# Two output tiles moved to the last phase of a two-branch attention kernel, and its closing steps put in another order

## The chip, the cores and the metric

The kernel runs on one core of a Trainium2 chip. The metric is the device time of one execution in microseconds. A core has a matrix engine (PE, with its weight loads listed apart as PEld), a vector engine (DVE), a scalar engine (ACT), GpSimd (POOL) and a sync engine (SP), which here issues every DMA. Each works through its own list of instructions in order, and they wait for each other by semaphores.

## The reference

Two attention branches over 2048 tokens, each 640 wide with 32 heads of 20 columns, side by side in the output. Branch A works in four segments of 512 tokens with a memory that is carried from one to the next; branch B has a sliding window of 256.

```python
# branch A, segment s (L = 512); M, z start at zero
p = softmax(qs @ ks.T * scale + causal_mask)
a_dot = p @ vs
a_mem = (phi(qs) @ M) / (phi(qs) @ z + 1e-6)      # phi(t) = t + 1 if t > 0 else exp(t)
o = g * a_mem + (1 - g) * a_dot                   # g = sigmoid(beta), one per head
M = M + phi(ks).T @ vs;  z = z + phi(ks).sum(tokens)
out_A = concat(o) @ wo

# branch B
mask = (i - j >= 0) & (i - j < 256)
out_B = softmax(where(mask, q @ k.T * scale, -1e9)) @ v @ wo

out = concat([out_A, out_B], axis=-1)
```

## The kernel before

The work is cut into chunks of 512 tokens and runs in eight **phases**, in the order B0, A0, B1, A1, B2, A2, B3, A3 (branch and chunk). The fourth phase is A1, the sixth A2, the seventh B3 and the last A3. A phase is a list of **packs**, 20 of them (24 in B1 to B3). A pack is one call of `scores`: PE writes the scores of four heads into two PSUM tiles called `Sc` (three buffers), ACT takes their exponential into `pt` with two instructions (L465), and POOL clears the masked blocks. The packs of all phases are counted by `slot`.

Around the packs, all other work is placed by a planner in `body`. Each kind of step has a cost in it: 0.45 a pack, 1.19 a projection of queries or keys (`proj`, L267), 0.79 half a projection of values (`vproj`, L326), 0.4 a step of the memory (`read`, L435, and `upd`, L402), 0.75 a sum of values for four heads (`weigh`, L514), and 0.75 half an output tile (`out_half`, L580). The planner adds these up to a total for the phase, and after each pack `pick` chooses how many of the next projections, memory steps and output halves to emit, so that the cost placed so far follows the share of the phase that is done. The projections of a phase are those of the next chunk, so the last phase has none.

All of these steps put their PSUM result into tiles called `D`, of which there are two buffers, and DVE takes nearly all of these results out, so PE and DVE hand the two buffers back and forth. A sum (`weigh`) of one group of four heads is copied to `oc` by DVE (L527), turned by a DMA transpose into `ocT`, and some packs later normalised (L544, L549) into `otA` or `otB`, the tokens' rows of a chunk; in branch A the memory's part `omem` is added (L561).

An **output tile** is 128 tokens of a chunk and a branch. `prefetch` issues a DMA transpose for it (L571, tile `oT`, up to three tiles under way), and at least two packs later `out_step` emits its halves: five matmuls with the weights `Ao` or `Bo` into a `D` tile and a DVE copy to `ot` (L583); behind the second half stands the store (L587). `OUT_TILES` says how many tiles each phase takes. There are 28 tiles of the first seven phases; the last phase asks for eight and gets the seven that are left. The four tiles of the last phase itself are made in the end, `tail`.

**The end** begins in the last pack. `last_turn` turns the first three of the five blocks of `otA` on PE (L616) ahead of that pack's scores and copies them to `pkt` (`oTs`, L623); after the pack `tail` emits, in this order: the sum of the last group but one (`weigh(u)`), its DVE copy, the last masks on DVE (L744), then for tile 0 the partial output over three of five blocks (`last_mm`, L628), the transposes of that sum on PE (`turn_here`, L536) and its normalisation, the partial output of tile 1, the last sum (`weigh(w)`), whose copy is split between ACT (L522) and DVE (L523), the partial output of tile 2, the transposes of the last sum and its normalisation. Then `last_turn` turns the last two blocks (L616) and copies them, half by DVE (L620) and half by ACT (L621). Three tiles are completed (two more blocks each), copied by ACT or DVE (L641, L643) and stored; the fourth is done whole, in an `Sc` tile, copied by DVE (640 columns) and stored by SP.

Of the kernel before, what the change touches and what calls it, by code (L numbers as in the profile page):

```python
# [9 lines left out]
BF16 = mybir.dt.bfloat16  # L10
F32 = mybir.dt.float32

P = 128
S = 2048
D = 640
# [4 lines left out]
KT = 5  # L20
NC = 4
CH = 512
CT = CH // P
# [1 line left out]
EPS = 1e-6  # L25
SCALE = float(DH) ** -0.5
LAG = 2
OUT_TILES = (0, 0, 3, 2, 6, 3, 7, 8)
VW = 22


# [51 lines left out]
class Kern:  # L83
# [411 lines left out]
    def weigh(self, u):  # L495
        nc = self.nc
        O = self.dtile([P, CH], F32)
        written = [False] * CT
        jobs = []
        for (_, kt, off, q0, nq), pt in u.work:  # L500
            runs = []
            for b in range(nq):
                w = written[q0 + b]
                if runs and runs[-1][2] == w:
                    runs[-1][1] += 1
                else:
                    runs.append([b, 1, w])
                written[q0 + b] = True
            jobs += [(kt, off + b, q0 + b, nb, pt) for b, nb, _ in runs]
        for n, (kt, off, q0, nq, pt) in enumerate(jobs):  # L510
            v = self.vt[u.br][(kt // CT) % 2 if u.br == "B" else 0]
            for j in range(4):
                v0 = VW * (4 * u.g + j)
                nc.tensor.matmul(O[32 * j:32 * j + 32, q0 * P:(q0 + nq) * P],  # L514
                                 lhsT=v[:, kt % CT, v0:v0 + 32],
                                 rhs=pt[:, j, off * P:(off + nq) * P],
                                 start=(n == 0), stop=(n == len(jobs) - 1),
                                 tile_position=(0, 32 * j))
        oc = self.wk.tile([P, CH], BF16, name="oc", bufs=2)
        if self.closing:  # L520
            if u.g == G - 1:
                nc.scalar.copy(out=oc[:, 0:256], in_=O[:, 0:256])  # L522
                nc.vector.tensor_copy(out=oc[:, 256:512], in_=O[:, 256:512])  # L523
            else:
                nc.vector.tensor_copy(out=oc[:], in_=O[:])
            return oc
        nc.vector.tensor_copy(out=oc[:], in_=O[:])  # L527
        tp = self.wk.tile([P, CT, P], BF16, name="ocT", bufs=4)
        nc.sync.dma_start_transpose(out=tp[:], in_=oc[:])
        late = 3 if u.br == "A" and u.c == NC - 1 else 4  # L530
        self.at(self.slot + late, lambda: self.normalise(u, tp))

    def turn_here(self, u, oc):
        tp = self.dtile([P, CT, P], BF16)
        for b in range(CT):
            self.nc.tensor.transpose(out=tp[:, b, :], in_=oc[:, b * P:(b + 1) * P],  # L536
                                     identity=self.ident[:])
        self.normalise(u, tp)

# [65 lines left out]
    def last_turn(self, br, c, m0, m1):  # L605

        nc = self.nc
        o = self.o_tok[br, c]
        if m0 == 0:
            self.oTs = self.wk.tile([P, KT, CT, P], BF16, name="pkt", bufs=1)  # L610
        n = 2 if m0 == 0 else 4
        for a in range(0, CT, n):
            ps = self.dtile([P, m1 - m0, n, P], BF16)
            for i in range(n):
                for m in range(m0, m1):
                    nc.tensor.transpose(out=ps[:, m - m0, i, :],  # L616
                                        in_=o[:, a + i, m * P:(m + 1) * P],
                                        identity=self.ident[:])
            if m0:
                nc.vector.tensor_copy(out=self.oTs[:, m0:m1, 0:2, :], in_=ps[:, :, 0:2, :])  # L620
                nc.scalar.copy(out=self.oTs[:, m0:m1, 2:4, :], in_=ps[:, :, 2:4, :])  # L621
            else:
                nc.vector.tensor_copy(out=self.oTs[:, m0:m1, a:a + 2, :], in_=ps[:])  # L623

    def last_mm(self, br, tt, m0, m1):
        for hf in range(2):
            for m in range(m0, m1):
                self.nc.tensor.matmul(self.last[tt][hf], lhsT=self.oTs[:, m, tt, :],  # L628
                                      rhs=self.w[br + "o"][:, m, hf * 320:(hf + 1) * 320],
                                      start=(m == 0), stop=(m == KT - 1))  # L630

# [4 lines left out]

    def last_store(self, br, c, tt, ps, eng):
        nc = self.nc
        ot = self.wk.tile([P, 2, 320], BF16, name="ot" if tt < 3 else "oT", bufs=3 if tt < 3 else 4)
        if eng is nc.scalar:  # L640
            nc.scalar.copy(out=ot[:], in_=ps[:, :, 0:320])  # L641
        else:
            nc.vector.tensor_copy(out=ot[:], in_=ps[:, :, 0:320])  # L643
        r0 = c * CH + tt * P
        c0 = 0 if br == "A" else D
        nc.sync.dma_start(out=self.out2d[r0:r0 + P, c0:c0 + D],
                          in_=ot[:].rearrange("p a b -> p (a b)"))

# [5 lines left out]
    def body(self):  # L656
# [4 lines left out]
        for n, ph in enumerate(phases):  # L661
            dense = lists[n]
            mem = []
            if ph.br == "A" and ph.c > 0:
                mem = [(0.4, lambda tt=tt, hf=hf: self.read(ph.c, tt, hf))
                       for hf in range(2) for tt in range(CT)] + upd[ph.c]
            outs = 2 * OUT_TILES[n]
            np_ = len(ph.packs)
# [67 lines left out]
    def tail(self, br, c):  # L736

        nc = self.nc
        self.closing, self.last, ps = True, {}, {}
        (_, u), (_, w) = self.ready  # L740
        assert not self.tiles
        ou = self.weigh(u)
        for blk in self.open_masks:
            nc.vector.tensor_tensor(out=blk, in0=blk,  # L744
                                    in1=self.cmask[:].unsqueeze(1).to_broadcast([P, 2, P]),
                                    op=ALU.mult)
        while self.turned or self.half:
            self.out_step()
        while self.after or self.behind:
            for f in self.after.pop(self.slot, []) + self.behind.pop(self.slot, []):  # L750
                f()
            self.slot += 1
        ps[0] = self.last_sc(0)
        self.last_mm(br, 0, 0, 3)
        self.turn_here(u, ou)
        ps[1] = self.last_sc(1)
        self.last_mm(br, 1, 0, 3)
        ow = self.weigh(w)
        ps[2] = self.last_sc(2)
        self.last_mm(br, 2, 0, 3)  # L760
        self.turn_here(w, ow)
        self.last_turn(br, c, 3, KT)
        for tt in range(3):
            self.last_mm(br, tt, 3, KT)
            self.last_store(br, c, tt, ps[tt], (nc.scalar, nc.vector)[tt % 2])
        ps[3] = self.last_sc(3)
        self.last_mm(br, 3, 0, KT)
        self.last_store(br, c, 3, ps[3], nc.vector)


@with_exitstack
# [47 lines left out]
```

## Time and profile before

| what | us |
|---|---|
| median of 3 runs | 392.48 (390.49 to 394.0) |
| the profiled execution | 390.19 |
| its span, first to last instruction | 388.1 |
| PE busy | 340.4 (88%) |
| ACT busy | 338.1 (87%) |
| DVE busy | 276.7 (71%) |
| POOL busy | 251.8 (65%) |

The span is what the profiler saw between the first and the last instruction of the core; the profiled execution's own time is 2.1 us more. "Busy" sums the time of an engine's instructions, and an average over the whole span says little here, since the phases differ in what sets their pace. In a line of waits, the engine and line before the arrow sat idle until the one behind it was done; the numbers are the total in us, how often, and the longest. In a line of the timeline stand the start, the duration, the engine, the line of the kernel, the operation and its output and input, the number of instructions that are merged in it, and in brackets the engine's idle time before it with what ended that.

### The profile page before, as it was taken

Reading aid. Unit: us, or ns where it says so; the run is one execution under the profiler, and the core shown is the slowest. Engines: PE = TensorE matmul, PEld = TensorE weight load, DVE = VectorE, ACT = ScalarE, POOL = GpSimd, SP = SyncE. Lnnn points to the kernel's source line nnn. Section 1 sums busy time; section 2 is a strip of 40 time slices with the busy share of each in tenths; the row PEclk is TensorE's granted clock in tenths of the full one; section 3 lists DMA queues with packets and bytes.
Section 4 is the critical chain, followed back from the end, with each engine's and each line's share of the span. In section 5 each row is a group of like instructions: output and inputs, shape, how many; then the busy total and the mean of one; then the engine's idle time right before and its main releaser. Section 6 shows DMA issues by size and latency. Waiting matters only on the chain.

```text
span 388.1 us, 10554 instructions
## 1 busy us (share of the span) xinstructions
PE 340.4 (88%) x4060; PEld 161.3 (42%) x4060; DVE 276.7 (71%) x581; ACT 338.1 (87%) x384; POOL 251.8 (65%) x392
## 2 busy tenths in 40 slices
PE   7999988977998798988997989898999989988884
PEld 3433434322443344444543335444454435544442
DVE  2467667634788868788778886789877887777583
ACT  2867789985999889888999999988999999999972
POOL 9657564542777587635578888844458988955550
PEclk9999999998999989999999999999999999999999
DMA  8993328647434597728575697758474377736312
GB/s 256 314 285 77 47 83 151 113 105 187 134 80 134 143 173 141 135 71 137 117 135 135 127 190 126 149 104 110 116 146 120 92 169 129 113 78 113 96 30 70
DMA packets 110738, 50.77 MB, mean 131 GB/s; under 512 B 81760, under 2 KB 110688, under 8 KB 110688
## 3 DMA queue, kind: packets, MB, share of 16 engines
q1 hardware_dynamic: 110688, 50.10, 61.1%
q8 instruction: 32, 0.52, 0.6%
q14 instruction: 18, 0.15, 0.1%
HBM read 16.39 MB, written 14.42 MB: 79 GB/s over the span
## 4 chain that ended last, share of the span: by engine, by line
PE 42%; ACT 24%; DVE 16%; issue 6%; POOL 6%; DMA 3%; SPq 0%; POOLq 0%; DVEq 0%; ACTq 0%
ACT pt L465 22%; PE D L267 13%; PE Sc L459 7%; PE D L326 6%; PE D L580 5%; PE D L514 5%; PE D L253 4%; POOL pt L479 3%; DVE qk L270 3%; POOL pt L485 3%; DVE oc L527 3%; ACT pe L310 2%; PE Sc L628 2%; DVE omem L445 1%; DMA ocT<-oc 1%
## 5 line engine op out<-in xcount | busy, mean ns | idle before, releaser
L465 ACT ACTIVATE pt<-Sc 128x1024 bf16<-128x1024 f32 (+1 forms) x344 | 320.7, 1077 | 32.3 <-PE Sc L459 28.2
L479 POOL TENSOR_SCALAR_AFFINE_SELECT pt<-pt 128x512 bf16<-128x512 bf16 x254 | 167.6, 671 | 117.2 <-ACT pt L465 116.9
L485 POOL TENSOR_SCALAR_AFFINE_SELECT pt<-pt 128x512 bf16<-128x512 bf16 x112 | 78.6, 717 | 5.1 <-ACT pt L465 4.8
L270 DVE CAST qk<-D 128x512 bf16<-128x512 f32 x70 | 47.9, 687 | 29.4 <-PE D L267 26.8
L527 DVE CAST oc<-D 128x512 bf16<-128x512 f32 x62 | 42.7, 688 | 19.9 <-PE D L514 19.8
L459 PE MATMUL Sc<-qpB,kpB 20*128 20x256 bf16 (+2 forms) x704 | 43.3, 277 | 7.8 <-ACT pt L465 4.7
L459 PE MATMUL Sc<-qpA,kpA 20*128 20x384 bf16 (+3 forms) x512 | 41.0, 302 | 5.8 <-ACT pt L465 5.0
L580 PEld LDWEIGHTS <-oT 128*128 128x128 bf16 x280 | 25.4, 98 | 17.9 <-issue 6.6
L583 DVE CAST ot<-D 128x320 bf16<-128x320 f32 x56 | 27.0, 485 | 7.2 <-PE D L580 6.4
L459 PEld LDWEIGHTS <-kpB 20*128 20x128 bf16 x704 | 13.6, 92 | 42.5 <-issue 38.5
L267 PE MATMUL D<-xTA,Aq 128*128 128x512 bf16 x100 | 24.9, 379 | 4.6 <-DVE oc L527 3.5
L326 PE MATMUL D<-Av,xTA 128*128 128x320 bf16 x160 | 26.2, 300 | 2.8 <-DVE vA L334 1.6
L514 PE MATMUL D<-pt,vA 128*32 128x256 bf16 (+3 forms) x576 | 23.5, 287 | 5.7 <-DVE qk L270 2.2
L580 PE MATMUL D<-Bo,oT 128*128 128x320 bf16 x160 | 27.3, 306 | 1.0 <-DVE omem L445 0.4
L267 PE MATMUL D<-xTA,Ak 128*128 128x512 bf16 x100 | 25.3, 384 | 2.1 <-DVE qk L270 2.0
L326 PE MATMUL D<-Bv,xTB 128*128 128x320 bf16 x160 | 26.0, 300 | 1.4 <-DVE oc L527 0.9
L514 PE MATMUL D<-pt,vB 128*32 128x384 bf16 (+2 forms) x720 | 26.1, 277 | 0.5 <-DVE qk L270 0.3
L459 PEld LDWEIGHTS <-kpA 20*128 20x128 bf16 x512 | 11.7, 91 | 30.6 <-issue 27.9
L267 PE MATMUL D<-xTB,Bq 128*128 128x512 bf16 x75 | 19.8, 396 | 3.4 <-DVE qk L270 3.2
L549 DVE TENSOR_TENSOR otB<-ocT,rr 128x320 bf16<-128x320 bf16 x32 | 20.2, 631 | 1.1
L544 DVE RECIPROCAL rr<-ocT 128x16 f32<-128x16 bf16 x62 | 15.1, 243 | 8.0 <-DMA ocT<-oc 8.0
L580 PE MATMUL D<-Ao,oT 128*128 128x320 bf16 x120 | 20.1, 299 | 0.7 <-DVE qk L270 0.4
(84 smaller groups left out, 358.8 us busy)
## 6 DMA issues: line engine op xcount, KB each, us to landing
out_dram<-ot SPq DMA_DIRECT2D x31, 160.0 KB
kdA<-qk SPq DMA_DIRECT2D x20, 128.0 KB
qdA<-qk SPq DMA_DIRECT2D x20, 128.0 KB
kdB<-qk SPq DMA_DIRECT2D x15, 128.0 KB
qdB<-qk SPq DMA_DIRECT2D x15, 128.0 KB
kpB<-kdB SPq DMA_DIRECT2D x8, 160.0 KB
qpB<-qdB SPq DMA_DIRECT2D x8, 160.0 KB
kpA<-kdA SPq DMA_DIRECT2D x8, 160.0 KB
```

The source lines that it names most:

```text
L267: nc.tensor.matmul(ps[:], lhsT=self.w[br + which][:, kt, m * P:(m + 1) * P], rhs=self.xT[br][:, kt, :], start=(kt == 0), stop=(kt == KT - 1))
L270: nc.vector.tensor_copy(out=t[:], in_=ps[:])
L326: nc.tensor.matmul(ps[:, 0:320], lhsT=self.xT[br][:, kt, tt * P:(tt + 1) * P], rhs=self.w[br + "v"][:, kt, hf * 320:(hf + 1) * 320], start ...
L459: nc.tensor.matmul(ps[j // 2][:, j % 2, off * P:(off + nq) * P], lhsT=kp[rows, u.g, k0:k0 + P], rhs=self.qp[u.br][rows, u.g, q0 * P:(q0 + ...
L465: nc.scalar.activation(out=pt[:, 2 * hp:2 * hp + 2, 0:pk.used], in_=ps[hp][:, :, 0:pk.used], func=ACT.Exp, scale=SCALE)
L479: nc.gpsimd.affine_select(out=blk, in_=blk, pattern=[[0, 4], [1, P]], compare_op=ALU.is_ge, fill=0.0, base=0, channel_multiplier=-1)
L485: nc.gpsimd.affine_select(out=blk, in_=blk, pattern=[[0, 4], [-1, P]], compare_op=ALU.is_ge, fill=0.0, base=-1, channel_multiplier=1)
L514: nc.tensor.matmul(O[32 * j:32 * j + 32, q0 * P:(q0 + nq) * P], lhsT=v[:, kt % CT, v0:v0 + 32], rhs=pt[:, j, off * P:(off + nq) * P], star ...
L527: nc.vector.tensor_copy(out=oc[:], in_=O[:])
L549: nc.vector.tensor_tensor(out=o[:, :, cols].rearrange("p b (j e) -> p b j e", j=4), in0=pv[:, :, :, 0:DH], in1=rr[:].unsqueeze(3).to_broad ...
L580: nc.tensor.matmul(ps[:, 0:320], lhsT=st["oT"][:, m, :], rhs=self.w[br + "o"][:, m, hf * 320:(hf + 1) * 320], start=(m == 0), stop=(m == K ...
L583: nc.vector.tensor_copy(out=st["ot"][:, hf * 320:(hf + 1) * 320], in_=ps[:, 0:320])
```

## The change

Two numbers of `OUT_TILES` go down by one: the fourth phase takes one tile (two before), the sixth two (three). The last phase asks for ten instead of eight and gets the nine that are left.

In the end, five things change. The last sum stands right behind the transposes of the sum before it, ahead of the partial output of tile 1; that partial output is split, its first half ahead of the transposes of the last sum and its second half behind them, where the partial output of tile 2 also goes. The two halves of the last sum's copy go to two tiles. ACT's half of the copy of the last two blocks goes to a tile of its own (`oTl`, a buffer that was used for `phik`), and `last_mm` takes these blocks from there for tiles 2 and 3. The last output tile is made by the new `last_tile`: two halves in `D` tiles, the first copied by DVE and stored by SP, the second copied by ACT and stored by a DMA that ACT issues.

```diff
-OUT_TILES = (0, 0, 3, 2, 6, 3, 7, 8)
+OUT_TILES = (0, 0, 3, 1, 6, 2, 7, 10)
...
             if u.g == G - 1:
+                o2 = self.wk.tile([P, CH], BF16, name="oc", bufs=2)
                 nc.scalar.copy(out=oc[:, 0:256], in_=O[:, 0:256])
-                nc.vector.tensor_copy(out=oc[:, 256:512], in_=O[:, 256:512])
...
+                nc.vector.tensor_copy(out=o2[:, 256:512], in_=O[:, 256:512])
+                return [oc, oc, o2, o2]
...
+        else:
+            t = self.wk.tile([P, CH], BF16, name="phik", bufs=3)
+            self.oTl = t[:].rearrange("p (m i q) -> p m i q", m=2, i=2)
...
-                nc.scalar.copy(out=self.oTs[:, m0:m1, 2:4, :], in_=ps[:, :, 2:4, :])
+                nc.scalar.copy(out=self.oTl, in_=ps[:, :, 2:4, :])
...
-    def last_mm(self, br, tt, m0, m1):
-        for hf in range(2):
+    def last_mm(self, br, tt, m0, m1, halves=(0, 1)):
+        for hf in halves:
             for m in range(m0, m1):
-                self.nc.tensor.matmul(self.last[tt][hf], lhsT=self.oTs[:, m, tt, :],
+                oT = self.oTl[:, m - 3, tt - 2, :] if m > 2 and tt > 1 else self.oTs[:, m, tt, :]
+                self.nc.tensor.matmul(self.last[tt][hf], lhsT=oT,
...
+    def last_tile(self, br, c):
+
+        nc = self.nc
+        ps = [self.dtile([P, CH], F32) for _ in range(2)]
+        self.last[CT - 1] = [p[:, 0:320] for p in ps]
+        r0 = c * CH + (CT - 1) * P
+        c0 = 0 if br == "A" else D
+        for hf in range(2):
+            self.last_mm(br, CT - 1, 0, KT, (hf,))
+            ot = self.wk.tile([P, KT, P], BF16, name="oT", bufs=4)
+            ot = ot[:].rearrange("p m q -> p (m q)")[:, 0:320]
+            if hf == 0:
+                nc.vector.tensor_copy(out=ot, in_=ps[hf][:, 0:320])
+            else:
+                nc.scalar.copy(out=ot, in_=ps[hf][:, 0:320])
+            (nc.sync, nc.scalar)[hf].dma_start(
+                out=self.out2d[r0:r0 + P, c0 + 320 * hf:c0 + 320 * hf + 320], in_=ot)
...
         self.turn_here(u, ou)
+        ow = self.weigh(w)
         ps[1] = self.last_sc(1)
-        self.last_mm(br, 1, 0, 3)
-        ow = self.weigh(w)
+        self.last_mm(br, 1, 0, 3, (0,))
+        self.turn_here(w, ow)
+        self.last_mm(br, 1, 0, 3, (1,))
         ps[2] = self.last_sc(2)
         self.last_mm(br, 2, 0, 3)
-        self.turn_here(w, ow)
         self.last_turn(br, c, 3, KT)
         for tt in range(3):
             self.last_mm(br, tt, 3, KT)
             self.last_store(br, c, tt, ps[tt], (nc.scalar, nc.vector)[tt % 2])
-        ps[3] = self.last_sc(3)
-        self.last_mm(br, 3, 0, KT)
-        self.last_store(br, c, 3, ps[3], nc.vector)
+        self.last_tile(br, c)
```

More of the change, by code (lines that the diff above doesn't have):

```diff
@@ L521, in weigh @@
             if u.g == G - 1:
+                o2 = self.wk.tile([P, CH], BF16, name="oc", bufs=2)
                 nc.scalar.copy(out=oc[:, 0:256], in_=O[:, 0:256])
[L523 to L526, printed above, removed]
+                nc.vector.tensor_copy(out=o2[:, 256:512], in_=O[:, 256:512])
+                return [oc, oc, o2, o2]
+            nc.vector.tensor_copy(out=oc[:], in_=O[:])
+            return [oc] * CT
         nc.vector.tensor_copy(out=oc[:], in_=O[:])
@@ L535, in turn_here @@
         for b in range(CT):
-            self.nc.tensor.transpose(out=tp[:, b, :], in_=oc[:, b * P:(b + 1) * P],
+            self.nc.tensor.transpose(out=tp[:, b, :], in_=oc[b][:, b * P:(b + 1) * P],
                                      identity=self.ident[:])
@@ L638, in last_store @@
         nc = self.nc
-        ot = self.wk.tile([P, 2, 320], BF16, name="ot" if tt < 3 else "oT", bufs=3 if tt < 3 else 4)
+        ot = self.wk.tile([P, 2, 320], BF16, name="ot", bufs=3)
         if eng is nc.scalar:
```

## The prediction, made before the changed kernel had run

> **What bounds the kernel now.** I read the page first, then busy time by phase, then who waited for whom inside each phase, then the chain of waits, and last the timeline of the end. A pack is one `scores` call: two exp activations on ACT. Counting back from the last of the 344 exps gives the phase limits: the fourth phase runs from 157.30 to 198.85 us, the sixth from 249.00 to 291.30, the seventh to about 338.30, the eighth to 375.50.
>
> ```profile
> span 388.1 us, 10554 instructions
> 157.30:198.85 41.55, 37.60 (x453) 18.93 (x452) 32.50 (x81) 37.68 (x42) 21.25 (x33) 1.00 0.59 111
> 249.00:291.30 42.30, 38.86 (x462) 19.67 (x460) 34.02 (x81) 37.64 (x42) 21.37 (x33) 1.00 0.68 128
> 290.00:338.30 48.30, 46.05 (x549) 21.75 (x547) 37.35 (x71) 47.71 (x55) 42.30 (x64) 1.00 0.64 128
> 338.30:375.50 37.20, 31.17 (x402) 15.59 (x399) 27.96 (x67) 37.20 (x41) 23.06 (x36) 1.00 0.38 84
> 324.04 51.49 ACT L465 ACTIVATE pt<-Sc 128x1024 bf16<-128x1024 f32 x56
> ```
>
> The columns after the length are busy us of PE, PEld, DVE, ACT and POOL, then granted clock, DMA share and GB/s. From 324.04 to 375.53 us ACT never rests: 51.49 / 56 = 0.92 us an exp, 1.84 us a pack. There ACT sets the pace. In the fourth and sixth phases ACT rests for 41.55 - 37.68 = 3.9 us and 42.30 - 37.64 = 4.7 us, and the view of waits names what it waited for: the first line is of the fourth phase, the next two are of the sixth. The chain of waits in the sixth passes through output matmuls (L580).
>
> ```profile
> ACT pt L465 <- PE Sc L459: 3.8, 7, 0.9
> ...
> ACT pt L465 <- PE Sc L459: 3.9, 8, 0.9
> ...
> ACT pt L465 <- POOL pt L479: 0.8, 1, 0.8
> ...
> 272.01 0.68 PE D L580 x5
> ...
> 284.47 0.84 PE D L580 x5
> 285.31 0.33 PE Sc L459 x8
> ```
>
> So in both phases that lose a tile the next scores come late because PE, trading its two D buffers with DVE, has too much in front of them. In the last phase the wait runs the other way:
>
> ```profile
> PE Sc L459 <- ACT pt L465: 2.7, 8, 0.6
> PE D L514 <- DVE omem L445: 0.8, 1, 0.8
> PE D L580 <- DVE ot L583: 0.2, 1, 0.2
> ```
>
> **The two tiles that move.** A tile is two halves, each five matmuls and one DVE copy, plus a DMA transpose and a store on SP's queue.
>
> ```profile
> 338.78 0.84 PE L580 MATMUL D<-Ao,oT 128*128 128x320 bf16 x5
> 339.55 0.68 PE L459 MATMUL Sc<-qpA,kpA 20*128 20x384 bf16 x8
> ...
> L583 DVE CAST ot<-D 128x320 bf16<-128x320 f32 x56 | 27.0, 485 | 7.2 <-PE D L580 6.4
> ...
> L571 SPq DMA_TRANSPOSE oT<-otB x16: 1199/1222/2140, 71.7 to 361.3; - x16
> ```
>
> A half holds PE for 339.55 - 338.78 = 0.77 us and DVE for 0.485 us. Removing a tile is worth at most 2 x 0.77 = 1.54 us, at least nothing. What it is worth in practice can be read off, because the profile holds a twin. The planner's total of a phase is 0.45 a pack, 1.19 a projection, 0.79 a value half, 0.4 a memory step, 0.75 an output half and 0.75 a group of heads. For the fourth phase before that is 9.0 + 11.9 + 6.32 + 5.2 + 4 x 0.75 + 6.0 = 41.42; for the sixth, with 6 halves, 42.92. With one tile fewer the sixth has 41.42 as well, with the same kinds of step in the same lists, so `pick` lays it out as the fourth is laid out now. The fourth phase of the trace is therefore a measurement of the sixth after the change: 42.30 - 41.55 = 0.75 us, half of the 1.54, at the same ACT time (37.6). The rest is DVE's: where the chain goes through a DVE copy, taking PE work out shortens nothing. Giving the fourth phase 2 halves instead of 4 has no twin; I take the same 0.75, between 0 and 1.54. Working the planner's choices through, the last five packs of the fourth and the last three of the sixth keep as much work as they had, and ACT is without a gap from about there on, so the gain is made earlier and kept. The fifth and seventh phases do as many halves in the same packs; only which tile it is shifts. Together -1.5 us (0 to -3.1).
>
> The last phase takes four halves more, 18 for 14: PE gets 4 x 0.77 = 3.1 us, DVE 4 x 0.485 = 1.9. PE's busy time goes from 31.17 to about 34.3 of 37.20 us (92%), DVE's from 27.96 to 29.9 (80%). What hides it is ACT's own time; PE now spends 2.7 us waiting directly for ACT, which is less than 3.1. The nearest row is the seventh phase: PE busy 46.05 / 48.30 = 95%, DVE 77%, and ACT lost 48.30 - 47.71 = 0.59 us, 1.2%. The same share of 37.20 is 0.45 us, which I take. From below 0; from above all of PE's 3.1 plus a D wait per half of 0.2 to 0.8 (the rows above), some 6.3. Matmul busy share alone is a poor measure of room, says the Trainium skill (Perfetto Trace Analysis, Identifying the Most-Contended Engine), which looks at the weight loads; by it, at 15.59 of 37.20 here and 21.75 of 48.30 in the seventh, this cost would be nil and the sum below 0.45 us lower, and the seventh phase agrees as far as 95% busy starved ACT for only 0.59 us.
>
> SP's queue gets two more transposes (1.2 us each) and two more stores in a phase with a DMA share of 0.38; a transpose is issued two packs, 3.7 us, before its use. The order into the end changes once: the last tile's halves stand both in the third pack from the end (before: one each in the fourth and third from the end).
>
> ```profile
> 369.21 0.49 DVE ot L583
> ...
> 370.42 1.30 DVE otA L561
> 371.72 0.40 DVE ot L583
> ```
>
> Both copies, with the 1.30 us addition between them, already lie on the chain; now the addition can start a copy earlier and two copies follow it. The sum of the three is the same, so I cost it at nothing, give or take 0.1.
>
> **The end.** These are its steps as they ran:
>
> ```profile
> 375.73 0.48 DVE L744 TENSOR_TENSOR pt<-pt,cmask 128x256 bf16<-128x256 bf16 x2
> 375.87 0.40 PE L536 MATMUL D<-ident,oc 128*128 128x128 bf16 x4
> 377.01 0.73 PE L514 MATMUL D<-pt,vA 128*32 128x256 bf16 x20
> 377.12 0.32 DVE L561 TENSOR_TENSOR otA<-otA,omem 128x320 bf16<-128x320 bf16 x1
> 377.79 0.37 ACT L522 CAST oc<-D 128x256 bf16<-128x256 f32 x1 [2.26 <-PE D L514]
> 378.19 0.42 DVE L523 CAST oc<-D 128x256 bf16<-128x256 f32 x1 [0.75 <-ACT oc L522]
> 378.50 0.46 PE L536 MATMUL D<-ident,oc 128*128 128x128 bf16 x4
> 379.00 0.26 DVE L544 RECIPROCAL rr<-D 128x16 f32<-128x16 bf16 x1 [0.38 <-PE D L536]
> 379.82 0.32 DVE L561 TENSOR_TENSOR otA<-otA,omem 128x320 bf16<-128x320 bf16 x1
> 380.20 0.56 PE L616 MATMUL D<-ident,otA 128*128 128x128 bf16 x7 [1.18 <-DVE otA L561]
> 380.80 0.42 DVE L620 COPY pkt<-D 128x512 bf16<-128x512 bf16 x1 [0.66 <-PE D L616]
> 381.26 0.58 ACT L621 COPY pkt<-D 128x512 bf16<-128x512 bf16 x1 [3.10 <-DVE pkt L620]
> 381.28 3.16 PE L628 MATMUL Sc<-Ao,pkt 128*128 128x320 bf16 x22 [0.52 <-DVE pkt L620]
> 382.04 0.69 ACT L641 CAST ot<-Sc 128x640 bf16<-128x640 f32 x1 [0.19 <-PE Sc L628]
> 384.48 0.82 DVE L643 CAST oT<-Sc 128x640 bf16<-128x640 f32 x1 [1.08 <-PE Sc L628]
> 385.33 0.33 SPq L646 DMA_DIRECT2D out_dram<-oT  x1
> ```
>
> Step 1: the last sum, `weigh(w)`, moves ahead of the six partial outputs of tile 1. Its masks are done at 375.73 + 0.48 = 376.21 and the transposes before it at 376.27, so it runs from 376.28 to 377.01 instead of from 377.01: 0.73 us earlier. Step 2: its two halves now have tiles of their own, so DVE no longer waits 0.75 us for ACT's half. But DVE is now at the addition that ends at 377.12 + 0.32 = 377.44, so its copy starts at 377.48, not at 377.05; against 378.19 that is 0.71 earlier, and the three partial matmuls that stand behind the sum fit in between. Of the two repairs together 0.71 stays, as each would have given most of it alone. Step 3: the transposes end 0.71 earlier, at 378.25, the normalisation (379.00 to 380.14 now) at 379.43. PE now has nine partial matmuls there, which stood ahead of the transposes before: 9 x 3.16 / 22 = 1.29 us, to 379.54, so PE, no longer DVE, is what ends last, by 0.1. With one more transpose ahead the seven start at 379.62 instead of 380.20: 0.58 earlier. Step 4: ACT's copy into its own tile no longer waits for DVE's, but its data was ready before use anyway (ended 381.84; the ninth matmul starts at 381.28 + 8 x 0.144 = 382.43): nothing. Step 5: the 22 matmuls end 0.58 earlier, near 383.86. The last eviction was 0.82 us on DVE for 640 columns; now it is 320 columns on ACT, between ACT's rows for 256 (0.37) and 640 (0.69): 0.42, 0.40 less. The first half's copy on DVE and its store on SP are done under the last five matmuls. Both halves use D buffers, which are free since the copies at 381. Step 6: the store itself:
>
> ```profile
> SPq L814 <- DMA out_dram<-oT: 1.4, 1, 1.4
> 386.00:387.00 1.00, 0.00 (x0) 0.00 (x0) 0.00 (x0) 0.00 (x0) 0.00 (x0) 1.00 0.47 164
> ```
>
> From the issue's end to the landing 1.4 us pass. A store of half the bytes, now issued by ACT, shows nowhere; it could save half of a movement that reaches about 0.5 us into this second, say 0.5, or cost as much as ACT's first issue may take beyond SP's 0.33, another 0.5. I take nothing. In the Trainium skill (DMA: Bandwidth & Descriptors, Issuing engines are not separate DMA queues) a second issuing engine saves only issue time; by it the 0.5 gained from a second queue is out, and no row here has a store issued by ACT.
>
> The end gives 0.58 + 0.40 = 1.0 us (0.4 to 1.5).
>
> **The sum** against the profiled execution: its time is 390.19 us, the span's 388.1 and 2.1 around it. 390.19 - 1.5 + 0.45 - 1.0 = 388.1. That execution lies 2.3 us below the median of the runs (392.48), so the same 2.05 us taken from the median give 390.4.
>
> **Rivals.** First, the moved halves were worth their whole PE time, and the last phase hides them: -3.1 - 1.0 = -4.1, 386.1 by the profile and 388.4 by the median. For it: the two pieces of L580 in the chain are PE on both sides; against it the twin's 0.75. Chance 0.20. Second, on the other side: PE becomes the bound of the last phase. Each half costs 0.77 and up to 0.8 of waiting for a D buffer, as several of them now stand right behind a sum whose copy DVE has yet to make; 4 x 1.57 = 6.3, less PE's spare 2.7, is 3.6 us of ACT idle, and -1.5 - 1.0 + 3.6 = +1.1: 391.3 and 393.6. It decides once the added PE time and waits exceed 2.7 + 2.5 = 5.2 us. Against it, the seventh phase's 0.59. Chance 0.12. Third, the change doesn't do what it says: ACT would have been late anyway in both phases (the 0.75 belongs to other differences, such as the 0.8 us that ACT waits for POOL in the sixth), and PE's nine matmuls undo the earlier sum, so that the eviction's 0.4 alone is left, against 0.45 lost: 390.2 and 392.5. Chance 0.13. The forecast has 0.55.
>
> **The numbers.** The time is that of the forecast, 390.4. Its own range is 389.2 to 391.8. The range goes down past the first rival to 387.6, with some of the store's 0.5, and up to 393.0, past the third and into the second; the runs before differ by 3.5 us among themselves (390.49 to 394.0). About 1% (3.9 us) is what a measurement of this kernel can tell from no change. Faster by more than that needs the first rival (most of 0.20) or the good end of the forecast: 0.20. Slower by more needs the second with its D waits unrelieved: 0.10 with what I can't see. Within: 0.70.
>
> **What would show it.** Right: ACT's idle in the sixth phase falls by about 0.75 us and the phase takes some 41.5 us; the eighth keeps ACT at 1.84 us a pack with at most three short gaps; the last sum directly follows the four transposes; DVE's half of its copy waits for no ACT; from the last exp's end to the end of the span it takes 11.6 us instead of 12.6. Wrong: gaps of ACT behind output halves in the last phase that add up to over 2.5 us, a sixth phase no shorter than 42.3, or a last store that lands later than 1.7 us after its issue.

## The result, and the profile after

The changed kernel takes 388.33 us in the median of four runs (387.09 to 389.55); the kernel before, run beside it, 393.24. The ratio is 0.9883 with a 95% interval of 0.9836 to 0.993, so 2.8 to 6.4 us are gone. A second measurement of the same kernel, told below, gave 0.9917 (0.9876 to 0.9958). The forecast was 2.05 us and a time of 390.4. Every ratio, here and below, leaves out the runs that took over 1.5% longer than the fastest of their kernel.

The first fence has the page's first line and the windows of the changed kernel's fourth, sixth, seventh and eighth phases, with the same columns as before (length; busy us of PE, PEld, DVE, ACT and POOL; granted clock; DMA share; GB/s).

```profile
span 386.9 us, 10557 instructions
```

```profile
158.30:198.10 39.80, 36.21 (x442) 18.03 (x441) 32.03 (x78) 37.67 (x42) 21.74 (x33) 1.00 0.57 107
248.31:289.61 41.30, 37.45 (x452) 18.90 (x451) 32.39 (x80) 37.65 (x42) 21.21 (x33) 1.00 0.60 123
289.61:337.05 47.44, 45.18 (x542) 21.46 (x541) 36.28 (x69) 46.85 (x55) 42.35 (x64) 1.00 0.59 127
337.05:375.75 38.70, 34.35 (x415) 17.50 (x413) 29.17 (x70) 36.84 (x41) 22.41 (x35) 0.96 0.43 97
```

The fourth phase is 41.55 - 39.80 = 1.7 us shorter and the sixth 42.30 - 41.30 = 1.0, both at the ACT time that they had (37.7). The seventh has not moved: the row of 48.30 us in the prediction starts 1.3 us before that phase's first exp, and by the exps it was 47.43 us before. The eighth has become longer, 38.70 for 36.8 (again by the exps), and there the last column but two is not 1.00: the granted clock of PE. ACT's timeline has one gap in the whole phase, at 351.80:

```profile
322.30 27.66 ACT L465 ACTIVATE pt<-Sc 128x1024 bf16<-128x1024 f32 x30
351.80 23.94 ACT L465 ACTIVATE pt<-Sc 128x1024 bf16<-128x1024 f32 x26 [1.85 <-PE Sc L459]
```

What PE did around it, in windows of a microsecond, and then two lines of its timeline:

```profile
346.00:347.00 1.00, 0.69 (x8) 0.42 (x5) 0.96 (x3) 1.00 (x3) 0.58 (x1) 1.00 0.43 89
347.00:348.00 1.00, 0.65 (x10) 0.17 (x8) 0.93 (x4) 1.00 (x3) 0.89 (x2) 1.00 0.32 65
348.00:349.00 1.00, 0.56 (x12) 0.53 (x16) 0.69 (x2) 1.00 (x3) 0.64 (x1) 0.65 0.76 151
349.00:350.00 1.00, 1.00 (x18) 0.44 (x7) 0.25 (x1) 0.95 (x2) 0.00 (x0) 0.50 0.00 0
350.00:351.00 1.00, 1.00 (x5) 0.32 (x3) 0.44 (x1) 0.00 (x0) 0.92 (x2) 0.50 0.00 0
351.00:352.00 1.00, 1.00 (x12) 0.43 (x12) 0.79 (x3) 0.20 (x1) 0.30 (x1) 0.64 0.33 68
```

```profile
348.44 1.26 PE L514 MATMUL D<-pt,vA 128*32 128x256 bf16 x20 [0.79 <-DVE omem L445]
349.63 1.51 PE L581 MATMUL D<-Ao,oT 128*128 128x320 bf16 x5
```

For 3.4 us PE ran at half its clock (a **dip**, below): the 20 matmuls of a sum took 1.26 us for 0.73, an output half 1.51 for 0.85, and the next scores came 1.85 us late. The kernel before had the same wait ahead of the same sum, and no such dip there:

```profile
350.18 0.73 PE L514 MATMUL D<-pt,vA 128*32 128x256 bf16 x20 [0.79 <-DVE omem L445]
```

So this gap should come from the dip and not from an output half that found no room, which is tested below. The end, from the last exp (375.75) to the end of the span, takes 11.16 us for 12.57:

```profile
375.84 0.49 DVE L767 TENSOR_TENSOR pt<-pt,cmask 128x256 bf16<-128x256 bf16 x2
376.23 0.73 PE L514 MATMUL D<-pt,vA 128*32 128x256 bf16 x20
377.01 0.37 ACT L523 CAST oc<-D 128x256 bf16<-128x256 f32 x1 [1.27 <-PE D L514]
377.15 0.32 DVE L562 TENSOR_TENSOR otA<-otA,omem 128x320 bf16<-128x320 bf16 x1
377.41 0.42 DVE L524 CAST oc<-D 128x256 bf16<-128x256 f32 x1
377.89 0.28 PE L537 MATMUL D<-ident,oc 128*128 128x128 bf16 x2 [0.17 <-DVE oc L524]
378.02 1.39 PE L633 MATMUL Sc<-Ao,pkt 128*128 128x320 bf16 x9
379.24 0.74 PE L620 MATMUL D<-ident,otA 128*128 128x128 bf16 x8
380.48 0.58 ACT L625 COPY phik<-D 128x512 bf16<-128x512 bf16 x1 [3.10 <-DVE pkt L624]
380.50 1.26 PE L633 MATMUL Sc<-Ao,pkt 128*128 128x320 bf16 x8 [0.52 <-DVE pkt L624]
383.70 0.42 ACT L668 CAST oT<-D 128x320 bf16<-128x320 f32 x1 [0.67 <-PE D L633]
384.15 0.37 ACTq L669 DMA_DIRECT2D out_dram<-oT  x1
```

The last sum starts at 376.23 as worked out (376.28), the nine partial matmuls fill PE behind the transposes, the last eviction takes 0.42 us on ACT. One line speaks against the prediction: ACT's copy of the last two blocks (L625), now into a tile of its own, still sat idle until DVE's was done.

### The profile page after: what moved, and what is told of

Its sections match the earlier page's. It is cut to its first block, busy times and chain, and to the rows that moved or that the text cites. A ratio compares the mean times of both kernels' runs of the same rounds, so it can differ in the third digit from the quotient of the medians.

```text
span 386.9 us, 10557 instructions
## 1 busy us (share of the span) xinstructions
PE 343.0 (89%) x4060; PEld 162.3 (42%) x4060; DVE 274.9 (71%) x581; ACT 338.8 (88%) x385; POOL 251.7 (65%) x392
## 4 chain that ended last, share of the span: by engine, by line
PE 45%; ACT 23%; DVE 16%; issue 6%; POOL 5%; DMA 3%; SPq 0%; POOLq 0%; ACTq 0%; DVEq 0%
ACT pt L465 20%; PE D L267 13%; PE Sc L459 7%; PE D L326 6%; PE D L514 6%; PE D L581 5%; PE D L253 4%; DVE qk L270 3%; DMA ocT<-oc 3%; POOL pt L479 3%; ACT pe L310 3%; DVE oc L528 3%; POOL pt L485 2%; DVE omem L445 2%; PE D L210 1%
## 5 line engine op out<-in xcount | busy, mean ns | idle before, releaser
L459 PE MATMUL Sc<-qpB,kpB 20*128 20x256 bf16 (+2 forms) x704 | 44.2, 276 | 8.6 <-ACT pt L465 5.5
L459 PE MATMUL Sc<-qpA,kpA 20*128 20x384 bf16 (+3 forms) x512 | 40.2, 304 | 4.0 <-ACT pt L465 3.4
L267 PE MATMUL D<-xTA,Aq 128*128 128x512 bf16 x100 | 26.0, 392 | 4.6 <-DVE oc L528 3.5
L581 PE MATMUL D<-Bo,oT 128*128 128x320 bf16 x160 | 26.3, 300 | 0.5 <-DVE omem L445 0.3
L581 PE MATMUL D<-Ao,oT 128*128 128x320 bf16 x120 | 20.9, 307 | 1.0 <-DVE omem L445 0.6
L267 PE MATMUL D<-xTB,Bk 128*128 128x512 bf16 x75 | 19.7, 396 | 1.2 <-DVE omem L445 0.8
```

The lines of the kernel that those rows point to most:

```text
L267: nc.tensor.matmul(ps[:], lhsT=self.w[br + which][:, kt, m * P:(m + 1) * P], rhs=self.xT[br][:, kt, :], start=(kt == 0), stop=(kt == KT - 1))
L459: nc.tensor.matmul(ps[j // 2][:, j % 2, off * P:(off + nq) * P], lhsT=kp[rows, u.g, k0:k0 + P], rhs=self.qp[u.br][rows, u.g, q0 * P:(q0 + ...
L581: nc.tensor.matmul(ps[:, 0:320], lhsT=st["oT"][:, m, :], rhs=self.w[br + "o"][:, m, hf * 320:(hf + 1) * 320], start=(m == 0), stop=(m == K ...
```

## The experiments

The twelve experiments run the changed kernel once more and eleven kernels that were cut from the two at hand; each ratio is to runs of the kernel before on the same chip. A single run tells little here, since runs of one kernel differ by up to some 2% (see the last section). What a part does to its phase is read from the profile, from ACT's first exp of the phase to that of the next (a row of the timeline that holds several exps is divided evenly among them). With the same work and no dip this repeats to 0.15 us in the sixth phase, and in the fourth as long as it has four halves. "The end" is good to 0.05, since spans are given to 0.1. Those readings, collected for all kernels:

| kernel (halves in fourth, sixth, last) | fourth | sixth | last | end | ratio, 95% |
|---|---|---|---|---|---|
| before (4, 6, 14) | 41.52 | 42.32 | 36.78 | 12.57 | 1 |
| changed, first profile (2, 4, 18) | 39.82 | 41.30 | 38.69, clock dip | 11.16 | 0.9883 (0.9836 to 0.993) |
| changed, second profile | 39.82 | 41.40 | 37.35 | 12.13, dip | 0.9917 (0.9876 to 0.9958) |
| new end alone (4, 6, 14) | 41.52 | 42.30 | 37.82, dip | 11.29 | 0.9962 (0.9923 to 1.0002) |
| tiles alone (2, 4, 18) | 39.93 | 41.29 | 38.75, dip | 12.44 | 0.9949 (0.9914 to 0.9985) |
| sixth alone (4, 4, 16) | 41.52 | 41.28 | 37.35 | 13.99, dip | 0.9986 (0.9936 to 1.0035) |
| one tile more (0, 4, 20) | 39.45 | 41.28 | 39.69, dip | 11.02 | 0.9939 (0.9903 to 0.9976) |
| two more (0, 2, 22) | 40.75 | 39.53 | 38.62 | 11.23 | 0.995 (0.9907 to 0.9992) |
| sixth's to fifth (2, 2, 18) | 39.97 | 39.80 | 38.70, dip | 11.03 | 0.987 (0.9824 to 0.9916) |
| sixth's to last (2, 2, 20) | 39.81 | 39.54 | 38.16 | 11.03 | 0.9884 (0.9839 to 0.993) |
| last store by SP (2, 4, 18) | 40.45 | 41.28 | 37.34 | 11.12 | one run |
| order alone (4, 6, 14) | 41.52 | 42.19 | 36.77 | 11.77 | one run |
| last tile alone (4, 6, 14) | 41.54 | 42.21 | 37.97, dip | 12.16 | one run |
| own tiles alone (4, 6, 14) | 41.54 | 42.31 | 36.78 | 15.28, dip | one run |

### The two halves of the change, and the change again

The new end alone:

```diff
 (the changed kernel)
-OUT_TILES = (0, 0, 3, 1, 6, 2, 7, 10)
+OUT_TILES = (0, 0, 3, 2, 6, 3, 7, 8)
```

> The new end with the old distribution of tiles. Theory A (the forecast): the end is worth 1.0 us, ratio about 0.9975, and from the last exp's end to the end of the span it takes 11.6 us. Theory B (the trace after the change, part by part): 1.4 us, ratio 0.9965, 11.2 us. Theory C (the excess over the forecast lies in the end): over 2.5 us, ratio below 0.994. In all three the last phase keeps ACT at 1.84 us a pack.

Measured: 0.9962, whose interval takes in A and B alike, and 11.29 us for the end, so 1.3 us: by the end it is theory B, more than the forecast's 1.0 and far from C. The two tiles alone:

```diff
 (the kernel before)
-OUT_TILES = (0, 0, 3, 2, 6, 3, 7, 8)
+OUT_TILES = (0, 0, 3, 1, 6, 2, 7, 10)
```

> The old end with the two tiles moved. Theory A: -1.5 + 0.45 = -1.05 us, ratio 0.9973; the fourth and sixth phases 0.75 us shorter each. Theory B: the fourth 1.75 and the sixth 1.0 shorter, and the last phase pays nothing unless PE's granted clock dips there: -2.75 us, ratio 0.993; with a dip -0.9. Theory D (the last phase turned PE-bound): ACT gaps of over 1 us in the last phase at a granted clock of 1.00.

Measured: 0.9949, between A and B; the fourth phase 1.6 us shorter and the sixth 1.0, as in B, the last one longer by 2.0 with a dip of the clock from 349.2 to 352.6 us. In 389 us the two halves are 1.5 and 2.0 us, the whole between 3.3 and 4.6: they add up. The unaltered change, a second time:

> The changed kernel once more, unaltered, beside the two halves of the change. Theory A: the sum of the two, ratio 0.995. Theory B: 0.989 to 0.990. If the gap of 1.85 us that ACT had in the last phase comes from the distribution of work, it is there again at the same pack; if it comes from a dip of the granted clock, it is gone or elsewhere.

Measured: 0.9917, with an interval that takes in both theories; but this profile settles the gap. The clock stays at 1.00 through the last phase, and the gap of 1.85 us is gone; what is left of ACT's waiting, with the same distribution of work, is one wait of 0.4:

```profile
340.62:377.97 37.35, 33.00 (x419) 17.23 (x416) 29.52 (x71) 36.90 (x41) 22.46 (x35) 1.00 0.45 101
```

```profile
ACT pt L465 <- PE Sc L459: 0.4, 1, 0.4
```

So the four halves more cost the last phase 37.35 - 36.78 = 0.57 us, and the dip some 1.3 on top in the first profile. It is no part of the change: the new end alone, with the old 14 halves, has a dip in the same place and 37.82 us (the last section says what a dip hangs on). Theory D falls.

### A tile from one phase alone

```diff
 (the kernel before)
-OUT_TILES = (0, 0, 3, 2, 6, 3, 7, 8)
+OUT_TILES = (0, 0, 3, 2, 6, 2, 7, 9)
```

> The old end, with only the sixth phase's tile moved to the last phase. By the twin: the sixth phase 41.5 us instead of 42.3, the kernel 0.75 less 0.2 for the last phase, ratio 0.9986. Theory B: 41.3, 1.0 us, ratio 0.9975. If a tile is worth its whole PE time: 40.8, ratio 0.996.

Measured: 0.9986 with an interval that takes in 1, and a sixth phase of 41.28: as in the changed kernel (theory B), 0.25 below the twin's 41.5. The fourth phase stays at 41.52, so its 1.7 us belong to its own tile. The last phase, with 16 halves, is 0.57 us longer, as much as with 18; a dip fell into its last 1.5 us.

### Going further with the tiles

```diff
 (the changed kernel, three times)
-OUT_TILES = (0, 0, 3, 1, 6, 2, 7, 10)
+OUT_TILES = (0, 0, 3, 0, 6, 2, 7, 11)    # one tile more
+OUT_TILES = (0, 0, 3, 0, 6, 1, 7, 12)    # two more
+OUT_TILES = (0, 0, 3, 1, 6, 1, 7, 11)    # sixth's to last
```

> The changed kernel with the fourth phase's last tile given away too: 0 tiles there, 10 left for the last phase (20 halves). Theory B (a tile taken from a phase where PE keeps ACT waiting is worth PE's time, until ACT alone sets the pace; the last phase pays 0.3 us a tile): the fourth phase 38.3 us instead of 39.8, the last 37.8 at full clock instead of 37.35, the kernel 1.0 us below the changed one, ratio 0.989. Theory D (the last phase is full at 18 halves): it takes 1.5 us a tile, and the kernel gains nothing over the changed one, ratio 0.992.

> The fourth phase at 0 tiles and the sixth at 1, 11 tiles left for the last phase (22 halves). The sixth then has the 39.8 us that the fourth had with one tile, 1.5 less than with two. Theory B: the last phase's PE work is 34.35 + 3.1 = 37.4 us, over ACT's 36.8, so that it takes 38.5 to 39 at full clock: 1.5 us below the changed kernel, ratio 0.987. Theory D: the last phase takes over 40 us, and all that the sixth gains is lost: ratio 0.992 or above.

> The changed kernel with one more tile taken from the sixth phase and given to the last (20 halves). The sixth 39.6 us instead of 41.3; the last between the 37.35 of 18 halves and the 38.62 of 22, so about 38.0; 1.1 us below the changed kernel at equal clock, ratio 0.989.

The fourth phase's last tile brought 0.4 us (39.45), not 1.5, and in the second of these kernels, with the very same work, the phase took 40.75. With few halves this phase repeats to no better than 1.3 us (with two halves it took 39.8 to 40.0 in five profiles, and 40.45 in the kernel whose last store alone differs). In both pairs the difference is one wait of ACT, ahead of the sixteenth pack: none with 39.45 and 1.2 us with 40.75, 0.1 with 39.82 and 0.7 with 40.45. This is the longest of the four:

```profile
191.57 1.94 ACT L465 ACTIVATE pt<-Sc 128x1024 bf16<-128x1024 f32 x2 [1.21 <-PE Sc L459]
```

Behind it stands a DMA transpose that landed late. DVE's normalisation waited for it, the copy of a `D` tile behind that came late, and PE waited 1.6 us for the copy. This is what DVE waited for the transposes in the fourth phase, first with 39.45, then with 40.75 us; why one was late is open.

```profile
DVE rr L545 <- DMA ocT<-oc: 0.3, 1, 0.3
DVE rr L545 <- DMA ocT<-oc: 2.0, 1, 2.0
```

The sixth phase behaved: its second tile was worth 1.5 to 1.75 us (39.53, 39.54 and 39.80 in three kernels), by the twin once more, since the fourth with the same two halves had 39.82. The last phase, where no dip fell into it, took 36.78, 37.35, 38.16 and 38.62 us with 14, 18, 20 and 22 halves: these are the window of the phase and ACT's waits in it with 22, then the window with 20.

```profile
339.25:377.87 38.62, 34.14 (x435) 18.44 (x434) 30.56 (x74) 37.05 (x41) 22.72 (x35) 1.00 0.50 114
```

```profile
ACT pt L465 <- PE Sc L459: 1.6, 3, 0.8
```

```profile
339.61:377.77 38.16, 34.81 (x444) 17.94 (x443) 29.20 (x72) 36.87 (x41) 23.15 (x35) 1.00 0.49 107
```

That is 0.57 / 4 = 0.14 us for each of the first four halves beyond 14, and 1.27 / 4 = 0.32 for each of the next four, but it doesn't come evenly: ACT loses it in single waits, one of 0.4 us with 16 and with 18 halves, one of 1.3 with 20, three with 22. The turn to PE as the bound, which would be 0.77 a half, is not reached with 22: PE is busy for 34.14 of 38.62 us there. The ratios of the first two kernels, 0.9939 and 0.995, miss theory B's 0.989 and 0.987: the fourth phase had gained little or nothing. The third kernel gave 0.9884; its phases say 1 us less than the changed kernel's (1.75 gained, 38.16 - 37.35 = 0.8 paid), but the intervals overlap, so it isn't shown to be faster.

```diff
 (the changed kernel)
-OUT_TILES = (0, 0, 3, 1, 6, 2, 7, 10)
+OUT_TILES = (0, 0, 3, 1, 7, 1, 7, 10)    # sixth's to fifth
```

> The changed kernel with one more tile taken from the sixth phase and given to the fifth (1, 7, 1, 7 in the fourth to seventh, 9 left for the last as in the changed one). Theory B: the sixth 39.6 us instead of 41.3; the fifth, where ACT was idle for 0.9 of 50 us and PE busy for 87%, takes it for at most 0.3; 1.4 us below the changed kernel at equal clock, ratio 0.988. If the fifth pays the tile in full: no gain, 0.992.

Measured: 0.987, the lowest ratio of all, and again not apart from the changed kernel's. The fifth phase did not take the tile for 0.3 us: without a dip in it, it has 51.36 us for 50.14, 1.2 more. These are its waits for the scores, 0.7 of the 1.2, first before, then here:

```profile
ACT pt L465 <- PE Sc L459: 0.9, 1, 0.9
```

```profile
ACT pt L465 <- PE Sc L459: 1.6, 2, 1.0
```

### The parts of the end

The order alone, on the kernel before (the lines of the change in `tail` and `last_mm`'s `halves`, nothing else):

> The kernel before with the order of the end alone changed: the last sum ahead of tile 1's partial output, that output split, tile 2's behind the transposes; one tile for the copy's halves and the old last tile. By the forecast's step 2 (each of the two repairs gives most of the 0.71 alone): the sum ends 0.73 us earlier, ACT's half is done at once, DVE's half starts 0.7 earlier, and the end takes 12.57 - 0.6 to 0.9 = 11.7 to 12.0 us. If own tiles matter as much as order, 12.3.

Measured: 11.77 us for the end, 0.8 less. The last output tile alone (`last_tile` in place of the last three lines of `tail`):

> The kernel before with the last output tile alone made in the new way (two halves, the second copied by ACT). Forecast's step 5: the last eviction 0.42 instead of 0.82 us, the end 12.57 - 0.4 = 12.2 us. If half a store also lands earlier, down to 11.7.

Measured: 12.16, 0.4 less. The tiles of their own for the last sum's copy, alone:

```diff
 (the kernel before)
             if u.g == G - 1:
+                o2 = self.wk.tile([P, CH], BF16, name="oc", bufs=2)
                 nc.scalar.copy(out=oc[:, 0:256], in_=O[:, 0:256])
-                nc.vector.tensor_copy(out=oc[:, 256:512], in_=O[:, 256:512])
+                nc.vector.tensor_copy(out=o2[:, 256:512], in_=O[:, 256:512])
+                return [oc, oc, o2, o2]
```

> The kernel before with the two halves of the last sum's copy in tiles of their own and nothing else. The forecast held that each of the two repairs gives most of 0.71 us alone: then the end takes 11.9 to 12.1 us. Rival: in the old order PE is busy with tile 2's partial output until 378.66, 0.9 us after the sum's end, so that a copy done 0.4 us earlier only waits for PE: 12.5 to 12.6, nothing gained.

A dip of two windows fell on this kernel's end (15.28 us), so its length can't be read, but its order can, and it was foreseen by neither theory:

```profile
382.46 0.37 ACT L523 CAST oc<-D 128x256 bf16<-128x256 f32 x1 [4.93 <-PE D L514]
382.86 0.42 DVE L524 CAST oc<-D 128x256 bf16<-128x256 f32 x1 [1.95 <-ACT oc L523]
```

DVE still starts behind ACT, with two tiles to write to; it is ACT's copy that ends its wait, as it was before. What the two copies still share is the `D` tile that both read. So the wait isn't removed by this part of the change, in neither place (L625 above is the other). That it comes from the common source was not tried by itself. Last, the store:

```diff
 (the changed kernel)
-            (nc.sync, nc.scalar)[hf].dma_start(
+            nc.sync.dma_start(
```

> The changed kernel with the second half of the last tile stored by SP instead of ACT. If the issuing engine gains nothing (SP has nothing else left to issue), the end from the last exp to the span's end stays at 11.2 us. If ACT's issue costs or saves something, up to 0.4 us either way.

Measured: 11.12 us for the end, against 11.16: the issuing engine makes no difference that one profile shows. That agrees with what the Trainium skill says (DMA: Bandwidth & Descriptors, Issuing engines are not separate DMA queues).

## Why the prediction was right, and where it was wrong

The direction and the places were right: the fourth and sixth phases shorter at the same ACT time, a small loss in the last phase, the end shorter, all of it adding up. The sizes of two terms were too small, and both misses go the same way: the 388.3 us lie in the stated range, but below the forecast's own 389.2 to 391.8 and beside the first rival's 388.4 (the second measurement had 389.3). That rival's number came without its mechanism, which had 3.1 us from the two phases, nothing lost in the last and 1.0 from the end. Term by term, at full clock:

| term | forecast | measured |
|---|---|---|
| sixth phase, by its twin | -0.75 | -1.0 |
| fourth phase, "I take the same 0.75" | -0.75 | -1.7 |
| last phase | +0.45 | +0.57 |
| end | -1.0 | -1.4 |
| sum | -2.05 | -3.5 |

- **The twin** held: 41.55 forecast, 41.3 measured, and the next tile, forecast by the fourth phase's 39.8, gave 39.5 to 39.8. In the trace PE's steps in the sixth phase now stand in the order that the fourth had before, up to the seventeenth pack.
- **The fourth phase** is the step that failed. It had no twin, and I gave it the sixth's price. The prediction had itself worked out that the last five packs keep their work, so that what goes is taken from the first fifteen; it didn't count what that is. In the trace those hold one output half and one value half less than before, and two pieces of 0.8 us on PE would be the 1.6 to 1.7 that were measured in most profiles (1.1 in one, with the late transpose). That it is these two pieces is argued, not shown: the same count fits the sixth phase's two tiles (one piece, 1.0 us; two, 1.5 to 1.75), but not the fourth's last tile, where an output half and a memory step less brought 0.4 us at most. ACT's wait in the phase fell from 3.8 to 1.8 us:

```profile
ACT pt L465 <- PE Sc L459: 1.8, 5, 0.5
```

  For this phase the first rival, the whole PE time, was right; for the sixth phase's first tile it was not (1.0 of 1.54). What a tile costs a phase isn't one number: the sixth's first brought 1.0, its second 1.5 to 1.75, the fourth's first 1.1 to 1.7 and its last 0.4 at most.
- **The last phase**: the share of ACT's time lost in the seventh phase (1.2%, 0.45 us) gave nearly the right size; 0.57 came. As a share of the time it was in part luck: both are one wait of ACT, 0.6 us there and 0.4 here, and with two halves more the wait was 1.3, at another pack. By the weight loads alone nothing would have been lost, and here the row was the better guide than the Trainium skill's rule (Perfetto Trace Analysis, Identifying the Most-Contended Engine). PE was busy for 33.00 of 37.35 us, 88% and not the 92% forecast, and the second rival, PE as the bound, did not come about even with eight halves more.
- **The end**: the order gave 0.8 for a forecast of 0.58, the last tile 0.4 as worked out; moving the two output tiles takes another 0.1 off (12.44). I had charged the nine partial matmuls from the transposes' reported end, 378.25; they started at 378.02, before the reported end of the two transposes ahead of them (377.89 + 0.28). The store by ACT brought nothing, as taken.
- **Step 2** was wrong in its reason. The forecast had the tiles of their own end DVE's wait for ACT, and each repair worth most of the 0.71 alone. The wait stays; it doesn't show in the changed kernel because DVE's addition ends (377.47) where ACT's copy does (377.38). The order alone already gave its 0.8 with one tile for both halves.
- **The third rival**, that ACT was late anyway, is out for the fourth phase and for the sixth's second tile, after which ACT's waits for the scores came down from 3.6 to 1.6 us (both lines are of the sixth phase, first the changed kernel, then the one with two tiles more moved). For the sixth's first tile it isn't: those waits fell only from 3.9 to 3.6, and the rest of the 1.0 us is the wait of 0.8 that was put down to POOL and is gone. At least 0.28 of that wait was PE's doing too, since ACT was free from 259.24 on and PE began that pack's scores at 259.52 (two lines of the kernel before):

```profile
ACT pt L465 <- PE Sc L459: 3.6, 7, 0.9
ACT pt L465 <- PE Sc L459: 1.6, 5, 0.5
```

```profile
259.52 0.39 PE L459 MATMUL Sc<-qpA,kpA 20*128 20x512 bf16 x4
260.04 2.85 ACT L465 ACTIVATE pt<-Sc 128x1024 bf16<-128x1024 f32 x3 [0.79 <-POOL pt L479]
```

## What to carry to other kernels

Look for a stretch whose twin, with one piece of work less, the profile already holds; but price each stretch by its own twin, and don't hand a price on to another. Work goes best where another engine sets the pace; what it costs there comes as single waits, so go by those and not by busy shares alone. Two engines that copy parts of one PSUM tile may still go one after the other when they write to tiles of their own: read the wait, before counting on it.

## What the runs showed of the hardware

PE's granted clock falls to one half in stretches of 3.4 us, and a run has between two and seven of them before its end. In each of the 14 profiles the loss from 8 us on, summed over windows of 2 us with a clock below 0.97, is a multiple of 1.7 us of full clock, to 0.1: 3.4 in three of them (before is one), 5.1 in the changed kernel's first, 6.8 in six, 8.5 in two, 10.2 and 11.9. They fall on a few places that all these kernels share, near 55, 75, 92, 138, 214, 350 and 376 us, and which of those a run gets differs. They are most of the scatter between runs: a straight line through 132 runs of the ten kernels and measurements that have an interval or are the kernel before, with a constant for each, gives 2.2 us for 0.01 of mean clock, about 1 us a stretch, and takes the scatter from 1.6 to 1.0 us. At equal clock by that line the change is worth 3.6 us (plus or minus 1.0) in the first measurement and 2.7 (0.6) in the second, and the two halves 1.4 (0.7) and 2.1 (0.6).

Which places a run gets can be read from the same traces. The stretches of a run keep a grid: from one to the next is a whole number of windows of 3.413 us. Cut each run by its grid, and count the matmuls that start in a window, each as the columns that it moves times the share of the 128x128 array that it uses (`128*32 128x256` counts 256 x 32/128 = 64). Of 1,460 windows at full clock from 14 us on, the 41 with counts under 2,816 are all followed by a stretch at half clock; of the 1,369 with counts over 3,440 none is; of the 50 in between 14 are. The median is 5,440. This is a pattern in 14 traces and was not tried by an experiment. It does account for the dip in the last phase: some 8 us into it the kernel before and the changed one both have a place with a count of 2,458, if a window happens to begin there. In the changed kernel's first profile one began 8.1 us into the phase; in the kernel before they began at 6.7 and 10.1 us and count 3,996 and 4,480.

The Trainium skill (TensorE: Matmul & The Clock Gate, What's actually happening) has a gate that halves the clock after an idle window of about 3.4 us and works in such windows. The length agrees. By its busy time PE need not be idle for that: it was busy for 2.30 of the 3.41 us ahead of the stretch at 348 us.

```profile
344.89:348.30 3.41, 2.30 (x25) 1.00 (x22) 3.24 (x10) 3.41 (x5) 1.85 (x4) 1.00 0.44 108
```
